# Gate logits of the values: 64 keys by 32 columns per matmul, two beside each other, and one copy per unit

## The chip, the cores and the metric

The kernel runs on one core of one Trainium2 chip. The metric is device time in microseconds (us) of the whole program. The kernel before took 998.04 us as the median of 3 runs (997.68 to 999.22).

## The reference

The program is a windowed attention whose output goes into a mixture of experts. All inputs are float32.

```python
# q, k, v: (8 batches, 8 heads, 576 positions, 64)
scores = q @ k.T / 8           # each query sees itself and the 63 positions before it
attn   = softmax(scores)       # masked to that window
x      = (attn @ v)            # heads side by side: 4608 tokens x 512
logits = x @ w_gate            # 8 experts
noise_scale = log1p(exp(x @ w_noise))
noisy  = logits + noise_scale * noise
# the two highest experts of each token, softmax over the two
out[token] = sum over its 2 experts of weight * relu(x @ w1[e]) @ w2[e]
```

The gate needs x @ [w_gate, w_noise], 16 columns per token. Since x is attn @ v, head by head, the kernel takes another order: it multiplies each head's values with that head's 64 rows of [w_gate, w_noise], puts the 16 results per key and head beside the values, and lets the attention's second matmul average them with the same weights. Summed over the 8 heads, that gives the 16 logits of the token. The matmul with the gate's weights is what this change is about.

## The kernel before, in words

**Stages.** First the attention, in 36 units (`for j in range(NT + 3)`, line 1104). A unit is 64 query positions of two batches, all 8 heads, 128 rows in all. Then the expert work, expert after expert in chunks of tokens (the loop at line 1181), in which TensorE multiplies gathered tokens with each expert's w1 and w2. Some of the first expert's work is taken into the last units of the attention (`ahead`, line 1081).

**A unit in the attention.** The order on every engine is the order in which the loop issues; nothing is reordered by a planner. Turn j of the loop issues, for TensorE: `scores(j)` (line 318), `pv(j - 2)` (line 378), sometimes a placing of tokens in expert lists (line 608), `transp(j - 1)` (line 354), `logits(j)` (line 288). ScalarE gets the copy `soft_a(j)` (line 328), the exponent `soft_b(j - 1)` (line 346), eight scalings `norm_b(j - 3)` (line 399), `logits_copy(j)` (line 294) and, at the head of the next turn, the small `norm_a` (line 388). VectorE gets the select `soft_max(j)` (line 336), the maximum (line 341), the mask `apply_mask(j - 1)` (line 359), and in between the routing of tokens to experts (lines 527 to 600), which is drained a few instructions at a time. GpSimd subtracts the maximum (line 342). So a unit's softmax is spread over three turns, and several engines hand work round within a turn: the exponent of unit j-1 stands on ScalarE behind the copy of the scores of unit j; the transposes of unit j-1 stand on TensorE ahead of the logits of unit j, and these ahead of the scores of unit j+1.

**Transfers.** SyncE issues, in program order, the loads of q, k, v and of v transposed (lines 118, 122, 131, 137; 256 to 272 KB each), and the store of x (line 402). Loads are one to four units ahead. `load_vt(j + 2)` comes after `logits(j)` and waits for it, because it writes the buffer that `logits(j)` has read (two buffers, named vt).

**The gate's logits.** `vt` of a unit holds the values transposed: 128 rows (two heads' dimensions of 64), four blocks q (two batches u by two groups g of heads), and in each block 128 columns, which are two sets `a` of 64 keys. `wgx` holds, for each group g, 64 columns: set a by two heads x by 16, with zeros where a row belongs to the other head. `logits(j)` multiplies, for each of the four blocks, all 128 key columns (as weights) with all 64 columns of `wgx[:, g]`, into 64 columns of the PSUM bank `idle` (tile ps_g in the profile). Of each such 128 by 64 result only two quarters are used: rows 0 to 63 with the columns of a=0, and rows 64 to 127 with those of a=1. `logits_copy(j)` therefore copies with two ScalarE instructions of 64 rows by 128 elements, one per set, into slot 4 of the tile `VW` (vw in the profile). `pv(j)` reads it two turns later, and `gate` (line 416) sums over the heads. The rest of the bank `idle` holds other small results at columns 256 and up: ranks, counts, token placings and the warm-up.

Every float32 matmul of the source leaves two weight loads and two matmuls in the profile; the 144 matmuls of line 288 are 288 of each.

Of the kernel before, what the change touches and what calls it, by code (L numbers as in the profile page):

```python
# [13 lines left out]
AF = mybir.ActivationFunctionType  # L14
# [74 lines left out]
def tile_kernel(ctx, tc, qT, kT, vx, vT, wgx, noise, w1, w2, out):  # L89
    nc = tc.nc  # L90
# [21 lines left out]
    VW = [acon.tile([128, 2, 5, 2, 4, 17], F32, name=f"vw{j}") for j in range(NP)]  # L112
# [28 lines left out]
    wgx_sb = acon.tile([128, 2, 64], F32)  # L141
# [11 lines left out]
    idle = ps.tile([128, 512], F32, name="ps_g")  # L153
# [123 lines left out]
        return lag([(w2s[:, f], W2["h"][:, f], W2["l"][:, f]) for f in (0, 4, 1, 5, 2, 6, 3, 7)])  # L277


    VG = idle[:, 0:256].rearrange("p (n c) -> p n c", n=1)  # L280

    def logits(j):
        p = VG[:, 0]
        x = VT.pop(j)
        for u in range(2):
            for g in range(2):
                q = u * 2 + g
                nc.tensor.matmul(p[:, q * 64:q * 64 + 64], lhsT=x[:, q, :], rhs=wgx_sb[:, g], start=True, stop=True)

    def logits_copy(j):  # L290
        i, bp = divmod(j, NP)
        for a in range(2):
            h = slice(a * 64, a * 64 + 64)
            nc.scalar.activation(VW[bp][h, i % 2, 4, :, :, 0:16].rearrange("p u (g x) e -> p (u g) x e", x=2),
                                 VG[h, 0].rearrange("p (k a x e) -> p k a x e", a=2, x=2, e=16)[:, :, a], AF.Copy)

    ST, T, P, TP, PT, XT = {}, {}, {}, {}, {}, {}

# [149 lines left out]
    for k in (1, 2, 4, 8, 16, 32):  # L448
        n = min(k, NT - k)
# [654 lines left out]
    for j in range(NT + 3):  # L1104
# [17 lines left out]
        if W1G // 2 - 4 <= j < W1G // 2 + 4:  # L1122
            k = j - W1G // 2 + 4
# [22 lines left out]
        on(transp, j - 1)  # L1146
        ahead(2)
        on(logits, j)
        if j < NT - 2:
            load_vt(j + 2)  # L1150
        blanks(j)
        on(norm_b, j - 3, 1)
        on(apply_mask, j - 1)
        drain(rate(2))
        on(logits_copy, j)
        ahead(2)
        on(gate, j - 3)
# [203 lines left out]
```

## Time and profile before

| | |
|---|---|
| time, median of 3 runs | 998.04 us (997.68 to 999.22) |
| profiled execution, its own time | 997.35 us |
| its span, first to last instruction | 995.3 us |
| TensorE busy, share of the span | 956.3 us, 96% |
| VectorE, ScalarE, GpSimd | 69%, 53%, 32% |
| mean granted TensorE clock | 0.997 |
| attention, from the start to the last unit's logits | about 173 us |

PE is TensorE's matmuls, PEld its weight loads, DVE VectorE, ACT ScalarE, POOL GpSimd, SP SyncE. A row `L288 PE MATMUL ps_g<-wgx_sb,vt` is line 288 of the kernel: it writes ps_g and reads wgx_sb and vt. "Idle before" is the time in which that engine stood before the instruction, and the arrow names what ended it. "Issue" is standing that nothing in the profile explains. The means hide two very different stages: the attention, where four engines and the transfers are all nearly full, and the experts, where TensorE alone is.

### The profile page before, as it was taken

The page shows a single profiled execution, that of the slowest core. Times are in us where ns is not written, and L with a number is a line of the kernel's source. Part 1 is how long each engine was busy: PE and PEld are TensorE (multiplying, and loading weights), DVE is VectorE, ACT ScalarE, POOL GpSimd, SP SyncE. Part 2 cuts the span into 40 slices and gives each one's busy share as a digit, 9 for nine tenths or more (in the row PEclk, how much of TensorE's full clock was granted, in tenths as well). Part 3 has the DMA queues.
Part 4 walks back from the last instruction along what each step waited for, and adds up shares of the span by engine and source line. Part 5 has one row for each costly group of instructions (what it writes and reads, how often), then busy time and mean ns, then how long its engine had stood idle before and what let it go on. Part 6 is the DMA issues. An engine that isn't in the chain of part 4 may idle for free. (4 is left out here: it accounts for less than half of the span.)

```text
span 995.3 us, 21900 instructions
## 1 busy us (share of the span) xinstructions
PE 956.3 (96%) x8408; PEld 858.2 (86%) x8408; DVE 689.9 (69%) x1728; ACT 525.9 (53%) x1346; POOL 320.1 (32%) x442
## 2 busy tenths in 40 slices
PE   8788888999999999999999999999999999999996
PEld 8777787888879888989898989898989898989895
DVE  5688898763786777767766786668666867686730
ACT  4888877522455545544554455445544554455531
POOL 5346546122322414040414141413131323241303
PEclk9999999999999999999999999999999999999999
DMA  9989997894649456854584458454945494647304
GB/s 326 365 270 314 287 294 273 271 263 119 153 89 267 81 130 132 252 73 120 116 265 70 125 115 267 60 134 87 283 63 143 73 266 89 149 93 206 48 1 56
DMA packets 107810, 168.93 MB, mean 170 GB/s; under 512 B 13424, under 2 KB 57712, under 8 KB 105904
## 3 DMA queue, kind: packets, MB, share of 16 engines
q1 hardware_dynamic: 90544, 126.96, 41.7%
q0 software_dynamic: 17152, 40.48, 21.9%
q8 instruction: 68, 1.11, 0.5%
q14 instruction: 46, 0.38, 0.1%
HBM read 110.08 MB, written 57.32 MB: 168 GB/s over the span
## 5 line engine op out<-in xcount | busy, mean ns | idle before, releaser
L966 POOL DMA_INDIRECT out_dram<-xg,los x70 | 111.9, 1598 | 427.5 <-ACT xh L774 124.3
L900 ACT ACTIVATE hb<-tq 128x288 fp32r<-128x288 f32 (+1 forms) x168 | 76.9, 458 | 143.9 <-DVE tq L919 143.7
L1038 PE MATMUL ps_d<-w2h,hb 128*128 128x512 f32 x392 | 152.9, 390 | 0.0
L1039 PE MATMUL ps_d<-w2l,hb 128*128 128x512 f32 x392 | 152.8, 390 | 0.0
L1040 PE MATMUL ps_d<-w2h,hb 128*128 128x512 f32 x392 | 152.7, 390 | 0.0
L919 DVE TENSOR_TENSOR tq<-ps_z,tq 128x288 f32<-128x288 f32 (+1 forms) x168 | 79.2, 472 | 89.0 <-PE ps_z L890 88.5
L888 PE MATMUL ps_z<-xh,WH 128*128 128x288 f32 (+1 forms) x448 | 137.5, 307 | 0.9
L889 PE MATMUL ps_z<-xl,WH 128*128 128x288 f32 (+1 forms) x448 | 135.2, 302 | 0.0
L890 PE MATMUL ps_z<-xh,WL 128*128 128x288 f32 (+1 forms) x448 | 135.2, 302 | 0.0
L904 DVE SCALAR_TENSOR_TENSOR hb<-tq,hb 128x320 fp32r<-128x320 f32 (+2 forms) x168 | 75.6, 451 | 37.5 <-ACT hb L900 35.2
L888 PEld LDWEIGHTS ps_z<-xh,WH 128*128 128x128 f32 x448 | 84.0, 188 | 5.5 <-DVE tq L919 3.7
L1040 PEld LDWEIGHTS ps_d<-w2h,hb 128*128 128x128 f32 x392 | 73.6, 188 | 15.6
L1038 PEld LDWEIGHTS ps_d<-w2h,hb 128*128 128x128 f32 x392 | 73.6, 188 | 14.0
L1039 PEld LDWEIGHTS ps_d<-w2l,hb 128*128 128x128 f32 x392 | 73.6, 188 | 13.8
L889 PEld LDWEIGHTS ps_z<-xl,WH 128*128 128x128 f32 x448 | 84.1, 188 | 1.1
L890 PEld LDWEIGHTS ps_z<-xh,WL 128*128 128x128 f32 x448 | 84.1, 188 | 0.0
L698 POOL DMA_INDIRECT xg<-xrows,lxs x70 | 69.0, 986 | 23.2 <-issue 22.6
L782 ACT ACTIVATE xh<-tq 128x512 fp32r<-128x512 f32 (+1 forms) x70 | 42.7, 610 | 61.9 <-DVE tq L778 60.5
L235 DVE TENSOR_TENSOR WL<-ws,WH 128x512 fp32r<-128x512 f32 x112 | 67.2, 615 | 6.6 <-ACT WH L243 6.5
L399 ACT ACTIVATE x<-ps_o,r 128x80 f32<-128x80 f32 x288 | 67.0, 350 | 7.5 <-DVE r L389 7.2
L378 PE MATMUL ps_o<-vw,pt 64*64 64x85 f32 x2176 | 49.9, 235 | 12.7 <-issue 8.2
L342 POOL TENSOR_TENSOR t<-t,mx 128x512 f32<-128x512 f32 x36 | 38.8, 1078 | 70.8 <-DVE mx L341 49.2
(242 smaller groups left out, 2347.0 us busy)
## 6 DMA issues: line engine op xcount, KB each, us to landing
ws<-in_w_dram SPq DMA_DIRECT2D x14, 2048.0 KB, 11.5
xs<-xg SPq DMA_DIRECT2D x63, 256.0 KB, 3.4
vw<-in_vx_dram SPq DMA_DIRECT2D x36, 272.0 KB, 4.5
out_dram<-zero SPq DMA_DIRECT2D x38, 256.0 KB, 4.6
qc<-in_qT_dram SPq DMA_DIRECT2D x36, 256.0 KB, 4.8
KW<-in_kT_dram SPq DMA_DIRECT2D x36, 256.0 KB, 4.9
vt<-in_vT_dram SPq DMA_DIRECT2D x36, 256.0 KB, 4.6
xrows<-x SPq DMA_DIRECT2D x36, 256.0 KB, 4.9
```

What stands on the lines that cost most here:

```text
L235: eng.tensor_tensor(l, x, h.bitcast(F32), op=OP.subtract)
L698: nc.gpsimd.indirect_dma_start(out=XG[e, c, q][:m], out_offset=None, in_=X[:DUMP + seen.get((e, c), NT) * 128], in_offset=bass.IndirectOff ...
L888: nc.tensor.matmul(p[:, :n], lhsT=WH[:, a, k, w], rhs=xh[:, b, k, :n], start=first and k == 0, stop=False, **free)
L889: nc.tensor.matmul(p[:, :n], lhsT=WH[:, a, k, w], rhs=xl[:, b, k, :n], start=False, stop=False, **free)
L890: nc.tensor.matmul(p[:, :n], lhsT=WL[:, a, k, w], rhs=xh[:, b, k, :n], start=False, stop=(k == 1), **free)
L900: nc.scalar.activation(hh[:, f, a:b], src, AF.Relu)
L904: nc.vector.scalar_tensor_tensor(hl[:, f, a:m], src[:, :m - a], 0.0, hh[:, f, a:m].bitcast(F32), op0=OP.max, op1=OP.subtract)
L919: nc.vector.tensor_tensor(t, a[:, :n], t, op=OP.add)
L966: s = nc.gpsimd.indirect_dma_start(out=out[:(2 + seen.get((e, c), NT)) * 128], out_offset=bass.IndirectOffsetOnAxis(ap=LT[e, c][1][q][:m], ...
L1038: nc.tensor.matmul(p, lhsT=h, rhs=w2h[:, f, :], **a)
L1039: nc.tensor.matmul(p, lhsT=h, rhs=w2l[:, f, :], start=False, stop=False)
L1040: nc.tensor.matmul(p, lhsT=l, rhs=w2h[:, f, :], **b)
```

## The change

`logits` now issues eight matmuls in place of four. Each takes one set of 64 keys as weights (all 128 rows, 64 columns) and only that set's 32 columns of `wgx`; the set a=0 writes PSUM rows 0 to 63, a=1 rows 64 to 127, both into the same 32 columns, so the two stand beside each other in the array's columns. What was computed and never read is no longer computed. A unit's results fill 128 columns of the bank in place of 256, and lie so that one ScalarE instruction over 128 rows by 128 elements copies them all.

```diff
-    VG = idle[:, 0:256].rearrange("p (n c) -> p n c", n=1)
+    VG = idle[:, 0:128].rearrange("p (n c) -> p n c", n=1)
...
                 q = u * 2 + g
-                nc.tensor.matmul(p[:, q * 64:q * 64 + 64], lhsT=x[:, q, :], rhs=wgx_sb[:, g], start=True, stop=True)
+                for a in range(2):
+                    h = slice(a * 64, a * 64 + 64)
+                    nc.tensor.matmul(p[h, q * 32:q * 32 + 32], lhsT=x[:, q, h], rhs=wgx_sb[:, g, a * 32:a * 32 + 32],
+                                     start=True, stop=True)
...
     def logits_copy(j):
         i, bp = divmod(j, NP)
-        for a in range(2):
-            h = slice(a * 64, a * 64 + 64)
-            nc.scalar.activation(VW[bp][h, i % 2, 4, :, :, 0:16].rearrange("p u (g x) e -> p (u g) x e", x=2),
-                                 VG[h, 0].rearrange("p (k a x e) -> p k a x e", a=2, x=2, e=16)[:, :, a], AF.Copy)
+        nc.scalar.activation(VW[bp][:, i % 2, 4, :, :, 0:16].rearrange("p u (g x) e -> p (u g) x e", x=2),
+                             VG[:, 0].rearrange("p (k x e) -> p k x e", x=2, e=16), AF.Copy)
```

## Rows read from the trace of the kernel before

**Rows 1.** The page: busy time, share of the span and instructions.

```profile
PE 956.3 (96%) x8408; PEld 858.2 (86%) x8408; DVE 689.9 (69%) x1728; ACT 525.9 (53%) x1346; POOL 320.1 (32%) x442
```

**Rows 2.** Stretches: start:end, length, busy time, granted clock, DMA share, GB/s.

```profile
20.00:60.00 40.00, 32.57 (x854) 30.05 (x856) 27.11 (x49) 33.82 (x126) 16.12 (x20) 0.96 0.99 347
60.00:160.00 100.00, 86.20 (x2394) 78.04 (x2383) 88.95 (x227) 80.67 (x308) 54.79 (x62) 1.00 0.94 302
...
200.00:220.00 20.00, 20.00 (x113) 16.90 (x112) 12.65 (x53) 4.95 (x9) 5.51 (x5) 1.00 0.87 239
220.00:960.00 740.00, 736.57 (x4149) 661.93 (x4148) 517.99 (x1287) 370.86 (x796) 208.85 (x289) 1.00 0.58 139
```

**Rows 3.** Waits, 20 to 176 us: who, for whom, total, times, longest.

```profile
DVE t L336 <- ACT t L328: 5.6, 12, 0.8
DVE pt L359 <- PE ps_t L354: 5.0, 5, 2.5
...
ACT t L328 <- PE ps_s L318: 6.3, 14, 1.7
...
PE ps_o L378 <- issue: 8.2, 9, 2.9
PE ps_t L354 <- ACT p L346: 4.3, 9, 0.7
```

**Rows 4.** Timeline, 87.5 to 92.7 us: start, length, engine, line, operation, count.

```profile
88.16 0.62 ACT L346 ACTIVATE p<-t 128x512 f32<-128x512 f32 x1
...
88.83 0.42 PEld L354 LDWEIGHTS ps_t<-ident,p 128*128 128x128 f32 x4
...
89.22 0.97 PEld L288 LDWEIGHTS ps_g<-wgx_sb,vt 128*128 128x128 f32 x8
...
89.33 1.00 PE L288 MATMUL ps_g<-wgx_sb,vt 128*128 128x64 f32 x8
...
90.26 0.86 PEld L318 LDWEIGHTS ps_s<-KW,qc 64*64 64x64 f32 x32
90.26 1.10 PE L318 MATMUL ps_s<-KW,qc 64*64 64x128 f32 x32
90.28 1.22 DVE L359 TENSOR_TENSOR pt<-ps_t,maskT 128x1024 f32<-128x1024 f32 x1
...
90.37 0.56 ACT L294 ACTIVATE vw<-ps_g 64x128 f32<-64x128 f32 x2
...
91.49 0.60 ACT L328 ACTIVATE t<-ps_s 128x512 f32<-128x512 f32 x1 [0.36 <-PE ps_s L318]
91.57 1.26 PEld L378 LDWEIGHTS ps_o<-vw,pt 64*64 64x64 f32 x63 [0.45 <-ACT r L388]
...
91.99 0.62 ACT L346 ACTIVATE p<-t 128x512 f32<-128x512 f32 x1
```

**Rows 5.** Groups by line: busy us, mean ns of one, idle before.

```profile
L378 PEld LDWEIGHTS ps_o<-vw,pt 64*64 64x64 f32 x2176 | 45.0, 133 | 17.0 <-issue 9.3 <-ACT t L328 3.1 <-ACT WH L222 2.0
...
L288 PEld LDWEIGHTS ps_g<-wgx_sb,vt 128*128 128x128 f32 x288 | 35.5, 194 | 0.0
...
L294 ACT ACTIVATE vw<-ps_g 64x128 f32<-64x128 f32 x72 | 19.7, 274 | 18.9 <-PE ps_g L288 18.1
...
L388 ACT ACTIVATE r<-ps_o 128x8 f32<-128x8 f32 x36 | 6.4, 178 | 0.7
```

**Rows 6.** Timeline, 40.5 to 52 us, around TensorE's longest stand.

```profile
46.06 0.51 PE L378 MATMUL ps_o<-vw,pt 64*64 64x85 f32 x11 [2.90 <-issue]
...
47.00 1.60 PE L288 MATMUL ps_g<-wgx_sb,vt 128*128 128x64 f32 x8
...
48.53 1.99 PE L318 MATMUL ps_s<-KW,qc 64*64 64x128 f32 x32
```

**Rows 7.** A stretch just behind that stand, columns as in Rows 2.

```profile
48.00:50.00 2.00, 2.00 (x31) 1.88 (x34) 0.70 (x2) 1.33 (x6) 0.01 (x1) 0.50 0.99 356
```

**Rows 8.** Queues: packets, MB, share of the 16 DMA engines.

```profile
q8 instruction: 68, 1.11, 0.5%
```

## The prediction

> **What bounds the kernel now.** I read four views in turn: the page's totals, the stretches, the waits of the attention, and one unit's timeline. The totals [rows 1] say TensorE is 96% busy, and that hides two stages. From 200 us on it is full: 20.00 of 20 us, then 736.57 of 740 [rows 2]. What the attention gives back earlier therefore reaches the end one for one, and what doesn't shorten the attention is worth nothing. All of the change lies in the attention. There, from 60 to 160 us, TensorE works 86.2, VectorE 89.0 and ScalarE 80.7 of 100 us, and the transfers hold 0.94 of their engines [rows 2]: no single bound, but a round of hand-overs that each engine joins with little slack, VectorE with the least.
>
> The timeline shows the round [rows 4]. From one exponent (88.16) to the next (91.99) is 3.83 us: 0.67 to the transposes (88.83), 0.39 to the first weight load of the logits (89.22), 1.04 to that of the scores (90.26), 1.23 to ScalarE's copy of them (91.49), 0.50 to the next exponent. The logits hold 1.04 us of it. ScalarE stood 0.36 us before that copy, waiting for the scores. So in a unit of this kind the logits are on the path, though nothing that the round waits for reads them. The waits say how often: the copy waited for the scores 14 times, VectorE's select for the copy 12 times, VectorE's mask for the transposes 5 times, the transposes for the exponent 9 times [rows 3]. In the other units VectorE is behind: in the timeline the mask starts at 90.28, some 0.8 us after its transposes [rows 4].
>
> **TensorE, per unit.** Removed: eight loads of 128 columns and eight matmuls over 64. The eight loads take 0.97 us, the last one 0.19 [rows 4, 5], so they follow each other by (0.97 - 0.19) / 7 = 0.11; the loads, not the shorter streams, set that. Added: sixteen loads of 64 columns and sixteen matmuls over 32. Loads of 64 columns last 133 ns against 194 for 128 [rows 5], 61 ns less, so I take a step at half of 0.11, 0.056 us. The question is whether the two sets go beside each other. The 64-column loads of the second attention matmul come 63 in 1.26 us, 0.020 each, those of the scores 32 in 0.86, 0.027 each [rows 4]. One after another at 0.056 they would need 3.5 and 1.8 us. So tiles in different quarters of the array do load at the same time; two halves are not shown, but they are the nearest thing to it. I take two at a time: 8 x 0.056 = 0.45 us.
>
> To that come the changes of shape. The scores' first load stands 1.04 - 8 x 0.11 = 0.15 us behind where another logits step would start; that is the pause from full tiles to quarters. After the change there is such a pause ahead of the logits too. The first logits load now lies beside the last transpose, so I charge the pause and a little more, 0.20 us. New distance from transposes' end to scores: 0.20 + 0.45 + 0.15 = 0.80, against 1.04: 0.25 us less per unit. Bounds: with no new pause and the cheapest record seen, 16 x 0.020 + 0.15 = 0.47, a gain of 0.57; with halves that load one after another, 0.20 + 0.90 + 0.15 = 1.25, a loss of 0.21. Sixteen steps as long as now (0.11) would be 2.1 us, a loss of 1.1 per unit, but no 64-column load in the rows is near that.
>
> The Trainium skill (TensorEngine Tiling, Key Properties) says that changing the tiling mode, not just the tile, drains the engine. The 0.15 us pause above agrees. If a change of columns alone did not count as one, the gain would be 0.45 per unit and the sum about 2.4 us larger.
>
> **ScalarE, per unit.** Two copies of 64 rows by 128 elements take 0.56 together, 274 ns each [rows 4, 5]. One of 128 rows by 128 elements is bounded by 178 ns (8 elements, 128 rows [rows 5]) and 600 (512 elements [rows 4]); between them by length, 178 + 120 x 422 / 504 = 278. I take 0.28, as the row of the same length has it: 0.28 us less. By the bounds it is between 0.38 less and 0.04 more.
>
> **How much of it counts.** The two savings don't add up. Where the score copy waits for the scores, TensorE's 0.25 moves it and ScalarE's 0.28 only lengthens its standing; where ScalarE is behind, its 0.28 moves it. Either way about a quarter of a microsecond, if VectorE can use it. VectorE has the least idle time, so I count units in which it stood waiting for that copy: 12 [rows 3]. 12 x 0.25 = 3.0 us. Its 5 waits for transposes I don't add: half of their 5.0 us is one stand of 2.5, which is the stall told of next. In the other 24 units I count nothing: VectorE is late there by its own work.
>
> **Added instructions.** 144 more matmuls are 288 more loads and 288 more matmul records. TensorE's 2 x 8408 records [rows 1] against the 68 packets of queue q8 [rows 8] are 247 per packet; I take q8 to be its program (an inference), so 2.3 more packets are fetched. TensorE stood 8.2 us in 9 places for "issue" [rows 3], in the middle of runs of matmuls. From 20 to 160 us are 6487 records [rows 2], 26 packets: 0.32 us of standing for each, so +0.7 us.
>
> Nothing else is added: no new wait, no new transfer. The load of v transposed behind the logits is issued a quarter of a microsecond earlier, the loads move as many bytes in slightly less time, and none of the listed waits [rows 3] is for a transfer. The copy writes the same slot and is read two turns later.
>
> **Sum.** -3.0 + 0.7 = -2.3 us. The profiled execution took 997.35 and would take 995.05. It lay 0.69 under the median of 998.04, so against the median I predict 995.7.
>
> **Rivals.**
>
> *The halves don't go side by side.* Then the change doesn't do what it is described to do: +0.21 us per unit on TensorE; over the same 12 units +2.5, with the fetches +3.2: 1001.2. For it: no row has two halves of the array. Against it: the quarters overlap. Chance 0.07.
>
> The Trainium skill (TensorEngine Tiling, Instruction Overhead) speaks against this change: a matmul has some 60 cycles of overhead, those under 60 columns are no faster, and one should not split a dimension that is already small. By that rule sixteen matmuls over 32 columns cost as much each as over 64, and only the overlap can save time. The rows count against it as far as 0.020 us per record of 85 columns goes.
>
> *VectorE takes the gain.* What the copy gains is spent waiting for VectorE a few instructions later, and the transfers, at 0.99 of their engines from 20 to 60 us [rows 2], allow no quicker pace there. 0 to -1.4, plus 0.7: 997.3 to 998.7. For it: 89% busy, and the late mask. Against it: the 12 waits, 5.6 us. Chance 0.16.
>
> *Slower: a fetch that comes too late.* At 46 us TensorE stood 2.90 us for "issue" [rows 6]; behind it the granted clock was 0.50 (1.2 GHz) [rows 7], and that turn's logits took 1.60 in place of 1.00 and its scores 1.99 in place of 1.10 [rows 4, 6]. Price of one such stall: 2.9 + 0.6 + 0.9 = 4.4 us. More records per unit, at a faster pace, meet nearly full transfers. One more: -2.3 + 4.4 = +2.1, 1000.1; two, 1004.5. It decides from half a stall on, where the gain is gone. For it: nine stands already. Against it: only one of the nine was long. Chance 0.11.
>
> *Faster: that stall isn't met.* The fetches fall at other places in the units, and the one long stall goes: -2.3 - 4.4, 991.3. Chance 0.17.
>
> *Every unit gains.* If the round sets the pace in all 36 units: 36 x -0.25 + 0.7 = -8.3, 989.7. Against it: the late mask. Chance 0.07.
>
> **How the numbers follow.** The forecast has 0.42; its own range is 994.3 to 997.2 (8 to 17 units that count, or a gain per unit of 0.15 to 0.30). A measurement of this kernel tells no change from 2.0 us, 0.2%. Of the forecast's 0.42, 0.26 lies under 996.04. Faster: 0.26 + 0.17 + 0.07 = 0.50. Same: 0.16 + 0.16 = 0.32. Slower: 0.07 + 0.11 = 0.18. The range goes from 990.5, which takes in the stall not met, to 1001.3, which takes in one more stall and halves that don't overlap; left out are all units gaining and two or more stalls.
>
> **What would show it.** Loads of line 288: 576, in about 0.45 us per unit, in pairs a few ns apart; from the transposes' end to the scores 0.8 us. One copy of about 0.28 us per unit. Units like that at 88 us at 3.6 us in place of 3.83. VectorE's waits for the copy down by some 3 us, its busy time unchanged. Standing for "issue" about 9 us, with or without a stand near 3 us and a clock of 0.50 behind it. I am wrong if logits take 0.9 us or more per unit, if VectorE's waits stay at 5.6 us, or if the issue stands change the time by more than the units do.

## The result and the profile after

The changed kernel took 1002.6 us (median of 10 runs, 1000.51 to 1005.8), the kernel before 997.82 us (10 runs) beside it. The ratio is 1.0053, with a 95% interval of 1.0037 to 1.0070: 0.5% slower where 0.2% faster was forecast. A second set of 12 runs on another chip gave 1.0032 (1.0009 to 1.0054). Chips differ by up to 3 us for the same kernel (before: 997.7 on two of them, 1000.6 on two others), so below only ratios to the kernel before on the same chip are compared. The profiled execution of the changed kernel took 1005.8 us, the slowest of its ten runs; its last exponent starts at 181.0 us, 7.8 us later than before (173.2).

The unit itself became what the prediction said. The timeline of one unit after, columns as in [rows 4]:

```profile
89.59 0.42 PEld L355 LDWEIGHTS ps_t<-ident,p 128*128 128x128 f32 x4
...
90.18 0.55 PEld L290 LDWEIGHTS ps_g<-wgx_sb,vt 128*64 128x64 f32 x16 [0.17 <-issue]
90.18 0.66 PE L290 MATMUL ps_g<-wgx_sb,vt 128*64 128x32 f32 x16
90.77 0.86 PEld L319 LDWEIGHTS ps_s<-KW,qc 64*64 64x64 f32 x32
...
90.89 0.28 ACT L295 ACTIVATE vw<-ps_g 128x128 f32<-128x128 f32 x1 [0.72 <-PE ps_g L290]
```

From the first transpose load to the first logits load it is 0.59 us, where it was 0.39: the 0.20 charged for the change of shape. From there to the scores 0.59, where it was 1.04: 0.45 for eight steps of two halves beside each other, and the old pause of 0.15. One copy takes 0.28. But the waits of the attention, 20 to 176 us, to be held against [rows 3]:

```profile
ACT t L329 <- PE ps_s L319: 18.4, 21, 3.5
DVE t L337 <- ACT t L329: 12.9, 15, 4.0
PE ps_o L379 <- issue: 12.1, 12, 2.9
PE ps_s L319 <- issue: 5.8, 5, 2.1
...
PE ps_g L290 <- issue: 3.1, 4, 1.4
...
PE ps_t L355 <- issue: 0.4, 1, 0.4
```

Before, beside the 8.2 us of [rows 3], there was one more such wait:

```profile
PE ps_s L318 <- issue: 1.0, 1, 1.0
```

TensorE stands 21.4 us for "issue", in 22 places, where it stood 9.2 in 10. The others wait for it: ScalarE's copy waits 18.4 us for the scores (6.3 before), VectorE 12.9 us for the copy (5.6 before). Most of these stands lie within runs of like matmuls. In the next unit's logits the first record runs, and the other fifteen follow a microsecond later:

```profile
93.76 0.24 PE L290 MATMUL ps_g<-wgx_sb,vt 128*64 128x32 f32 x1
94.82 0.54 PEld L290 LDWEIGHTS ps_g<-wgx_sb,vt 128*64 128x64 f32 x15 [0.93 <-issue]
94.82 0.66 PE L290 MATMUL ps_g<-wgx_sb,vt 128*64 128x32 f32 x15 [0.82 <-issue]
```

The stretches after, columns as in [rows 2]. From 60 to 160 us TensorE is busy 79.7 us (86.2 before), VectorE 84.4 (89.0): every engine is busy for less of the same time. From 220 us on the kernels are alike. The last two stretches lie ahead of and behind a stand of 2.62 us that ends at 131.97; the row of that stand comes after them:

```profile
20.00:60.00 40.00, 31.07 (x909) 26.71 (x901) 26.86 (x48) 30.98 (x118) 16.01 (x20) 0.96 0.98 344
60.00:160.00 100.00, 79.74 (x2430) 68.81 (x2427) 84.38 (x213) 70.24 (x274) 52.84 (x60) 0.98 0.90 285
...
220.00:960.00 740.00, 736.55 (x4145) 661.50 (x4144) 520.59 (x1304) 368.87 (x791) 212.29 (x290) 1.00 0.59 142
```

```profile
128.00:131.00 3.00, 1.34 (x44) 1.19 (x41) 2.97 (x8) 1.98 (x7) 2.72 (x4) 1.00 0.99 302
132.00:134.50 2.50, 2.50 (x66) 2.31 (x66) 1.22 (x2) 1.58 (x8) 1.04 (x1) 0.50 0.39 143
```

```profile
131.97 2.54 PE L379 MATMUL ps_o<-vw,pt 64*64 64x85 f32 x64 [2.62 <-issue]
```

Behind the stand the granted clock is 0.50 (1.2 GHz), and the second attention matmul takes 2.54 us for 64 records where 1.4 is usual. The trace after has half clock for 17 us of the attention, in four stretches: three begin at such stands of 2.1 to 2.9 us, the fourth, at 175.9, behind waits of 1.3 and 1.5 us for VectorE. Before it was 3.4 us, once. A second profile of the changed kernel, of a run of 1002.28 us, has as much standing (21.7 us) but only 6.8 us at half clock. Over all runs the mean granted clock was 0.9913 after and 0.9945 to 0.995 before.

### The profile page after: what moved, and what is told of

It is laid out like the page before. It is cut to its first block, busy times and chain, and to the rows that moved or that the text cites. A ratio compares the mean times of both kernels' runs of the same rounds, so it can differ in the third digit from the quotient of the medians.

```text
span 1004.1 us, 22440 instructions
## 1 busy us (share of the span) xinstructions
PE 955.6 (95%) x8696; PEld 851.2 (85%) x8696; DVE 691.3 (69%) x1728; ACT 513.9 (51%) x1310; POOL 321.2 (32%) x442
## 3 DMA queue, kind: packets, MB, share of 16 engines
q0 software_dynamic: 17152, 40.48, 21.7%
## 5 line engine op out<-in xcount | busy, mean ns | idle before, releaser
L379 PE MATMUL ps_o<-vw,pt 64*64 64x85 f32 x2176 | 54.8, 245 | 14.2 <-issue 12.1
```

## The experiments

Three causes were held against each other. **Supply** (called fetch in the first expectations): TensorE's program comes in q8 packets; more records (a record is one weight load or matmul of the profile) need more packets, and these come late. **Clock:** TensorE has less work, so its clock is taken down. **Pace:** any quicker unit runs into the transfers and stands. Each kernel ran 12 times, against 29 to 35 runs of the kernel before on its chip. "Stands" below is the sum of TensorE's issue waits from 20 to 176 us in the one profiled execution of a kernel.

**Records added to the kernel before.**

```diff
+        for _ in range(8):
+            nc.tensor.matmul(idle[:, 484:485], lhsT=ones_b, rhs=ones_b[:, 0:1], start=True, stop=True)
```

> The kernel before, with eight bfloat16 matmuls of one column added behind each unit's logits (16 records, as many as the change adds; their result is read by nothing). Fetch theory: TensorE's program comes a packet of about 247 records at a time, and in the attention a packet takes about 5.4 us (29 intervals between q8 packets from 12.8 to 174.6 us in the kernel before), so records and not their work set the pace: 36 x 16 = 576 records, 2.3 packets, up to 12 us, less what hides behind other waits: 1003 to 1010, issue stands of TensorE from 20 to 180 us over 15 us (9 before, 21 after the change). Clock theory (shorter matmuls leave TensorE less busy, and its clock is then taken down): TensorE only gets busier, eight weight loads at 0.036 us are 0.3 us per unit, no more than 3.5 us over 12 units: 998 to 1001.5, no more stretches of half clock than before. Pace theory (any quicker unit runs into the transfers): nothing is quicker, as the clock theory.

Measured: 1.0018 (0.9997 to 1.0038), 999.07 against 997.76; stands 9.5 us. The mean clock over the runs rose to 0.9959. With range(16):

> The kernel before with sixteen bfloat16 matmuls of one column per unit in place of none (32 records, 0.6 us of TensorE work per unit; with eight it was 999.1). Supply theory: 4.7 packets more, stands over 15 us: 1003 to 1010. Clock theory: TensorE is busier, no half clock in the attention; what it costs is work, 0.6 us in the units where TensorE is on the path: 999 to 1004, stands no more than with eight (8.8 us).

Measured: 1.0049 (1.0028 to 1.0069); stands 8.1 us. Supply alone missed both, in the time and in the stands. The clock theory's times were met, but for 3.4 us at half clock in the second, where it had none. The time grew with the records, or with the up to 0.6 us of work per unit that came with them (these two can't tell), but not through stands. One reading is that work that comes with the records gives TensorE something to do while the next packet comes; the long streams below test it. The count of packets does follow the records. Queue q8 moved 68 packets before and 71 after, as with these 576 records; with 1152 added ones:

```profile
q8 instruction: 73, 1.20, 0.5%
```

**Half of the logits, without and with added records.** This pair separates records from work, since in it TensorE has less work than in either kernel.

```diff
-        for u in range(2):
+        for u in range(2 if j == 0 else 1):
...
+        for r in range(8):      # the second of the pair alone
+            h = slice(r % 2 * 64, r % 2 * 64 + 64)
+            nc.tensor.matmul(idle[h, 484:485], lhsT=ones_b[:, h], rhs=ones_b[:, 0:1], start=True, stop=True)
```

> The kernel after, but from the second unit on with the logits of the first batch alone: four matmuls in place of eight, 16 records per unit fewer, as many records as the kernel before. The logits of the second batch are left out. Fetch theory: 2.3 packets fewer than after, and shorter logits: 992 to 997, issue stands back to about 9 us. Clock theory: TensorE is less busy still, so as many half-clock stretches as after or more: 1002 or above. Pace theory: units are quicker still, so the transfers stop them more: 1002 or above.

> The half-logits variant of the kernel after, with eight bfloat16 matmuls of 64 keys by one column added per unit (16 records, two beside each other; nothing reads them). It has the records of the kernel after and less TensorE work, about 0.2 us per unit over the variant without them (996.1). Supply theory: 2.3 more packets, stands near those of after: 1000 to 1003. Clock theory: TensorE is a little busier than in the variant without them, half clock no more than there: 995 to 998.

Measured: 0.9998 (0.9980 to 1.0016) without, 996.12 us; 1.0051 (1.0031 to 1.0070) with, 1003.15 us. Sixteen records per unit of matmuls over a single column cost 0.53% by the ratios, 5.3 us (2.7 to 7.9; the medians, taken on two chips, differ by 7.0). TensorE's issue waits in the first and in the second:

```profile
PE ps_o L379 <- issue: 8.5, 11, 2.3
PE ps_s L319 <- issue: 2.4, 2, 1.4
```

```profile
PE ps_s L322 <- issue: 10.2, 9, 2.6
PE ps_o L382 <- issue: 9.0, 9, 2.3
PE ps_g L294 <- issue: 2.5, 2, 1.3
PE ps_g L290 <- issue: 1.6, 1, 1.6
```

10.9 us become 23.3, as from before to after. The first kernel also refutes the clock theory in its plain form, and pace as the cause of the loss: TensorE has the least work of all there, the clock is low (0.9903 over its runs), and the time is not above that of before. Nor is it below: beside the stands TensorE waits 21.9 us there (14.3 before) for other engines and for transfers, among them

```profile
PE ps_o L379 <- ACT t L329: 5.2, 6, 1.0
```

against 1.7 us before.

**The copies apart from the matmuls.** The one copy in the kernel before (`[:, :, 0]` of the same PSUM columns for all 128 rows), and the two copies in the kernel after:

> The kernel before with one ScalarE copy of 128 rows in place of two of 64 (it copies set 0 for all rows, so that half of the logits are those of the wrong set). TensorE's instructions are those of before. Fetch theory: the program is as long as before, ScalarE saves 0.28 us per unit: 995 to 998. Clock theory: as before or slightly faster, 995 to 998. Pace theory: quicker units bring stands: 999 to 1002.

> The kernel after with two ScalarE copies of 64 rows, as before. Fetch theory: the 576 added records remain: 1002 to 1006. Clock theory: the short matmuls remain: 1002 to 1006. Pace theory: units lose ScalarE's part of the gain, so fewer stands: 999 to 1002.

Measured: 0.9996 (0.9979 to 1.0014), and 1.0049 (1.0029 to 1.0069). ScalarE's saving is worth nothing that these runs can measure (their interval would hide 2 us), and the loss comes with the eight matmuls.

**Fewer loads.** In both kernels v transposed is loaded for two units alone:

```diff
-        VT[j] = ld.tile([128, 4, 128], F32, name="vt", bufs=2)
-        nc.sync.dma_start(VT[j], vT[bp, i])
+        if j < 2:
+            VT[j] = ld.tile([128, 4, 128], F32, name="vt", bufs=2)
+            nc.sync.dma_start(VT[j], vT[bp, i])
...
-        x = VT.pop(j)
+        x = VT[j % 2]
```

> The kernel before, with v transposed loaded for the first two units alone and those two used again in all others (34 loads of 256 KB left out, so the logits are those of other units). Supply theory (packets of TensorE's program come late because data loads fill the DMA engines): issue stands from 20 us to the last exponent fall from 8.7 us to under 4, no half-clock stretch, 988 to 995. Clock theory (what costs is half clock, which comes with little TensorE work): stands and half clock as before, 996 to 998.

> The kernel after with the same loads left out. Supply theory: stands fall from 20.9 us to under 8, and without them the shorter units show: 1 to 4 us faster than the same cut in the kernel before, 986 to 993. Clock theory: the short matmuls still let the clock fall: 3 to 6 us slower than the same cut in the kernel before.

Measured: before 0.9963 (0.9943 to 0.9983), 993.95 us; after 0.9975 (0.9954 to 0.9995), 994.89 us. From 60 to 160 us the transfers hold 0.83 of their engines in both, in place of 0.94 and 0.90. The stands fall to 5.9 us in the first; in the second 21.4 us become 7.2:

```profile
PE ps_s L320 <- issue: 3.4, 5, 1.1
PE ps_o L380 <- issue: 3.3, 6, 1.1
PE ps_g L291 <- issue: 0.5, 1, 0.5
```

Of the distance between the two kernels (0.53% and 0.32% in the two sets) 0.12% is left, within the intervals. So the added stands need nearly full transfers. The clock theory, which left the distance as it was, missed. Supply missed in part: after was not the faster of the two, as it should have been without stands, and the first kernel's stands were to fall under 4 us, and it kept 3.4 us at half clock. The mean clock of the second stayed lower (0.9919 against 0.995 over the runs).

**The same records, longer streams.** Each of the eight matmuls streams 128 columns in place of 32:

```diff
-                    nc.tensor.matmul(p[h, q * 32:q * 32 + 32], lhsT=x[:, q, h], rhs=wgx_sb[:, g, a * 32:a * 32 + 32],
-                                     start=True, stop=True)
+                    nc.tensor.matmul(p[h, 0:128], lhsT=x[:, q, h], rhs=wgx_sb.rearrange("p g c -> p (g c)"), start=True, stop=True)
```

> The changed kernel once more, beside the other two of this call. Both theories: 1001 to 1004, issue stands near 20 us up to the last exponent, mean clock about 0.991.

> The kernel after with the same eight matmuls, the same weight loads and as many records, but each streams 128 columns in place of 32, all into the bank's first 128 columns (so the logits are those of the last block). A step goes from 0.058 to about 0.11 us, a unit's logits from 0.45 to about 0.9 us, as in the kernel before. Supply theory alone (each late packet costs its stand, whatever TensorE does meanwhile): the longer units come on top, 1002 to 1006. Supply and clock together (packets come late against a TensorE that has little to do, and its stands then cost a halved clock as well): with the work back the stands shrink to about 9 us and half clock to under 5 us, as in the variant of the kernel before with as many records (999.1): 998 to 1001, faster than after though every unit has more work.

> The half-logits variant of the kernel after (16 records per unit, second batch left out) with each matmul streaming 128 columns in place of 32. With a_half (0.9983 to the kernel before on another chip is within its interval of 1), after and a_long it makes a square of records and work. Supply theory alone: few records, so no added stands, and the work costs nothing or up to 0.2 us in some units: 0.998 to 1.001 of the kernel before. Supply and clock together: the mean clock goes from 0.990 back to 0.995 or above, worth about 2 us: 0.995 to 0.999.

Measured: the changed kernel again 1.0032 (1.0009 to 1.0054), mean clock 0.9918, stands 21.7 us; with long streams 1.0016 (1.0001 to 1.0032), mean clock 0.9975, stands 11.0 us. The distance from the first logits matmul to the first of the scores went from 0.59 to 1.02 us, some 15 us more TensorE work over 36 units, and the kernel did not become slower. The stands halved, and that trace has no half clock in the attention. (1002.55 us itself fits either forecast, on a chip where the kernel before takes 1000.6.) In the half-logits variant the same edit gave 0.9981 (0.9961 to 1.0001; without it 0.9998), mean clock 0.9944 in place of 0.9903, so there as well more work cost nothing; but its stands, few already, did not fall (12.5 us, 10.9 without), and the two forecasts overlap at its time. The stretch from 60 to 160 us, columns as in [rows 2], in the half-logits variant with added records and in the long-stream variant:

```profile
60.00:160.00 100.00, 81.41 (x2422) 70.19 (x2415) 83.63 (x211) 69.66 (x273) 51.34 (x57) 0.93 0.88 278
```

```profile
60.00:160.00 100.00, 90.73 (x2527) 76.82 (x2525) 87.34 (x221) 72.74 (x280) 54.80 (x62) 1.00 0.95 299
```

Both have the records of the changed kernel. The one with more work per record gets through more records (2527 against 2422), at a granted clock of 1.00 against 0.93. The first of the two profiles is of that kernel's slowest run; over all runs the clocks are 0.9888 and 0.9975.

**The place of the packets' ends.** 64 bfloat16 matmuls of one column (half a packet) ahead of the first unit:

> The kernel after with 64 bfloat16 matmuls of one column (128 records, half a packet) ahead of the first unit; all later packets end half a packet elsewhere in the units. Chance of place (the change moved the packets' ends to bad places, and others would be good): some 3 us or more off the kernel after, either way, stands of another total. Supply theory: stands fall on other lines, their total stays near 20 us, 1002 to 1005.

Measured: 1.0009 (0.9992 to 1.0025), beside 1.0032 (1.0009 to 1.0054) of the changed kernel on the same chip; stands 14.5 us. The intervals overlap. By the middle values place would be worth 0.2%, most of the loss on this chip; this run neither shows nor excludes it. That records of a single column in place of the logits' brought the same loss (1.0051) speaks against place alone.

**The loads' time.** The constant W1G from 12 to 28, which puts the first expert's w1 eight units later:

> The kernel before with the eight loads of the first expert's w1 (2 MB) and their splits issued eight units later: out of the stretch from 20 to 60 us, where the transfers hold 0.99 of their engines, into one where they hold 0.94. Supply theory: the stand of 2.9 us at 46 us and the half clock behind it go or shrink, others come later: 0.996 to 1.000 of the kernel before. Clock theory: no change, 0.999 to 1.001.

> The same in the kernel after. Supply theory: a little faster than after, still behind the kernel before, because its stands are spread over the whole attention: 1.000 to 1.004 of the kernel before. If the fullest stretch alone made the stands: 0.996 to 0.999. Clock theory: as after, 1.003 to 1.006.

Measured: 1.0019 (1.0003 to 1.0034) and 1.0035 (1.0014 to 1.0057). The first is a miss: the kernel before became slightly slower, though its stands fell to 7.9 us. Emptying the fullest stretch (0.90 of the transfer engines from 20 to 60 us in place of 0.99) does not help; the changed kernel's stands (17.2 us) are spread over the whole attention.

**The packets in the trace.** The traces settle what the stands are. Number TensorE's instructions from 0 in order of start, weight loads, matmuls and waits for semaphores together. In the kernel after, 20 of the 22 stands (19.4 of 21.4 us) end at an instruction 193 + 256 n, always the same place in 256; before it is 7 of 10 (7.5 of 9.2 us), over all sixteen traces 205 of 260. A packet of q8 has 16 KB, 64 bytes for each of 256 instructions. So most stands, and nearly all of the changed kernel's, are at the edge of a packet of TensorE's program; the rest stay unexplained. From 20 to 176 us no such block's first instruction started sooner than 1.1 us after its packet had landed, in any trace; after, 23 of 29 start within 1.7 us of it, before 15 of 28. The transfer of one packet takes the same in every trace (median 0.94 to 0.97 us). What differs is how early it begins, measured to the last instruction of the block before: at the median 2.56 us before and 1.72 after, 3.22 and 2.37 with fewer loads, 2.09 with long streams.

No version that computes the whole result beat the kernel before. One copy with the old matmuls, had it a layout that keeps both sets, would be worth 0.9996 by what was seen.

## Why the prediction was wrong

**Right: the cost of each edit.** Two halves go beside each other, the step is as forecast, the new pause is 0.20 us, the distance from the transposes to the scores fell by 0.25 us net (0.20 more, 0.45 less), the copy takes 0.28 us. The rival that the halves don't overlap is out.

**The step that failed first: "How much of it counts".** It took the exponent's round for what paces the unit, and counted 12 waits of VectorE, 12 x 0.25 = 3.0 us. The runs show nothing of it. One copy with the old matmuls: 0.9996. Even half the logits with one copy and no added record: 0.9998. And 0.43 us more TensorE work per unit cost nothing. VectorE's waits for the copy, which were to fall by 3 us, rose from 5.6 to 12.9. Time freed on TensorE was spent in waits: with few records for the other engines and transfers (half the logits: 32.8 us of waits in all, 10.9 of them for issue), with many for the next packet (the changed kernel: 31.6 us, 21.4 for issue). So the rival "VectorE takes the gain" was right that the gain comes to nothing. [Rows 3] had the sign of the second kind: the longest waits of TensorE in the attention were not for ScalarE or VectorE but for "issue", 8.2 us.

**The step that was mis-sized: "Added instructions".** The term had the right mechanism, 2.3 more packets (three were counted), but took their price as the mean stand per packet, 0.32 us, 0.7 in all. That price was too low even where TensorE had work to cover the packet's coming: the long streams have the step of the kernel before (1.02 us, 1.04 before) and 576 records more, and cost 1.0016, 1.6 us (0.1 to 3.2), 0.7 us a packet. The change did both at once, more records and less work per record. The pair with half the logits gives the price without cover: 5.3 us (2.7 to 7.9) for 576 records, 2.3 us a packet, seven times the term; the lower clock that came with it is in it. "No new wait" failed as well, if only by a little: the logits now wait twice, 1.3 us in all, for the load of v transposed.

**The slower rival had the mechanism and the wrong shape.** "A fetch that comes too late" got 0.11 as one or two more stands of 2.9 us. There came twelve more stands, most of 0.2 to 1.5 us, and three more stretches of half clock, two of them at long stands. The time lies outside the range because the range took in one such event. (The forecast's own range, 994.3 to 997.2, does not quite come out of its counts either: they give 994.5 to 996.9.)

**What the clock adds.** Within one count of records, more TensorE work goes with a higher mean clock (0.9918 to 0.9975, 0.9903 to 0.9944) and a ratio lower by 0.0016 and 0.0017: some 1.6 us, though the intervals of each pair overlap. On the chip with all three, by the middle values, the records with cover cost 1.6 us (before to long streams) and taking the cover away another 1.6 (long streams to the changed kernel), stands and half clock together. How the second part divides between them is not shown. By the two rows of 64 records (2.54 us at half clock, 1.4 at full) 17 us of half clock hold up to 7.7 us of delay, an estimate and an upper bound: the half-logits kernel had 10.2 us of it in its trace and took 996.04 us.

**Open.** That q8 is TensorE's program, taken as an inference in the prediction, is borne out by the counts (68, 71, 71 and 73 packets for 0, 576, 576 and 1152 added records) and by the stands at every 256th instruction. That a late packet is one whose transfer begins late, and that fewer loads make it begin sooner, is shown; whether it is asked for late or waits in the queue, no run tells. Whether better places for the packets' ends would win back 0.2% is open as well.

## What to carry to other kernels

Ask of a change not only how long its instructions take but how many there are: in a stage that runs short instructions beside nearly full transfers, the program itself is a transfer, and issue stands within runs of like matmuls are its mark. Count the instructions between such stands: where the counts are multiples of one number, 256 here, the engine waits for its program. In this kernel splitting matmuls to shorten them shortened nothing, and longer ones, as many, cost nothing. Price an added instruction with the work that covers its coming, since an average stand per packet tells nothing of what a packet costs when that work goes.

## What the runs showed of the hardware that was not expected

In the half-logits kernel, eight more matmuls per unit of a single column each, with their loads, cost 5.3 us, while in the changed kernel 15 us of added streaming in as many instructions cost nothing. TensorE's program came in packets of 256 instructions, and in the attention the first instruction of a packet never started sooner than 1.1 us after the packet's landing. And the granted clock was lower in the kernels with less TensorE work in the attention: 0.989 to 0.993 as the mean over runs, against 0.994 to 0.998 in those with more.
